# Query and key projections of two linear-attention layers as seven block products over pairs of token tiles, with the weight sums kept in DRAM

## The chip, the cores and the metric

The kernel runs on one core of one Trainium2 chip. The metric is the device time of one execution in microseconds (us); a profile of one execution of each kernel was also taken, and its "span" is a little shorter than the timed execution. Ratios between two kernels are the mean time of one kernel's fast runs over the mean of the other's fast runs of the same rounds, so they are not quite the ratio of the medians that are quoted. The times of "before" drift by up to 2.3 us between the chips that the batches ran on, so I compare ratios first and spans second.

## The reference

Two rounds of two blocks on x of shape (1, 2048, 1024): a linear attention with 32 heads of 32, and a gated bilinear layer of width 3584. Cut to what matters:

```python
def _A_ref(x, wqkv, wo):                       # linear attention; runs twice
    q, k, v = split(x @ wqkv)                  # x is layer-normalised; 32 heads of 32
    phi = lambda t: jnp.where(t > 0, t + 1, jnp.exp(t)) + 1e-6
    pq, pk = phi(q), phi(k)
    kv = jnp.einsum("bhsd,bhse->bhde", pk, v)
    z = jnp.einsum("bhsd->bhd", pk)            # sum of the keys over the tokens
    o = (pq @ kv) / (pq . z + 1e-6)
    return o @ wo
def _B_ref(x, w_gate, w_up, w_down):           # runs twice
    return ((x @ w_gate) * (x @ w_up)) @ w_down

x = x + A(layernorm(x)); x = x + B(layernorm(x))
x = x + A(layernorm(x)); x = x + B(layernorm(x))
```

I call the two attention blocks "layer one" and "layer two". In each the order of stages is: projections of q and k (with phi), state products, output products. After each come a first gate/up pass, a first down pass, and a second of both.

## The kernel before

Tokens are cut into 16 tiles of 128. For every tile and each half (512 columns) of q and k, eight 128x512 matmuls run into one PSUM bank; phi then needs one exponential on ACT (ScalarE), and a clamp and a combination on DVE (VectorE). A running sum of the keys for z is added up on Pool (GpSimd).

```python
def phi_evac(bank, dst_ap, dst_rng, eng):               # eng is "dve" everywhere
    er = R(O_E[r], 2048)                                # f32 buffer
    act:  e.activation(etmp[r], psb(bank), AF.Exp)
    eng:  e.tensor_scalar(out=etmp[r], in0=etmp[r], scalar1=1.0, scalar2=1e-6, op0=ALU.min, op1=ALU.add)
    dve:  e.scalar_tensor_tensor(out=dst_ap, in0=psb(bank), scalar=0.0, in1=etmp[r], op0=ALU.max, op1=ALU.add)

def proj(w, base, i, h, dst, r_dst, eng):
    pe:   [e.matmul(psb(bank), xnT[:, k, i*128:(i+1)*128], w[:, k, h*512:(h+1)*512], ...) for k in range(8)]

def proj_k(i, h):
    proj(wk, ...)()
    pool: e.tensor_tensor(out=za, in0=za, in1=pk[:, h, i, :], op=ALU.add)     # sum of keys, f32
...
for kind, i in seq:                                     # k tile i and q tile i-2, alternating
    ...                                                 # layernorm steps of later tiles in between
    if first and i >= 3:
        pack()                                          # DRAM to DRAM: gate/up weights into a dense order,
                                                        # 28 packings in all, 2 x 256 KB each
```

(The excerpt is shortened: buffers and dependency ranges are cut.) The first gate/up pass then runs 28 units on a ring of five weight slots; it loads each packed unit, makes its block sums on DVE and stores them for later passes, and also prepares the down weights. So its DMA engines have much to do.

## Time and profile before

1485.99 us, median of 3 runs (1485.0 to 1490.21). What matters:

| stage | us in the profile |
|---|---|
| layer one, first projection to first state product | 8.0 to 119.0 |
| layer one, output products begin | 192.4 |
| first gate/up pass | 248.5 to 417.7 |
| layer two, projections | 756.6 to 860.2 |
| layer two, output products begin | 930.5 |

The first lines of the page of the kernel before (busy time of each engine, share of the span and number of instructions; then the chain of waits that ended last, by engine):

```profile
span 1483.7 us, 20453 instructions
...
PE 1462.0 (99%) x7597; PEld 730.2 (49%) x7662; DVE 1148.6 (77%) x2122; ACT 538.7 (36%) x1096; POOL 214.2 (14%) x239
...
PE 79%; DVE 11%; DMA 5%; issue 2%; POOL 1%; ACT 1%; SPq 0%; DVEq 0%; ACTq 0%; POOLq 0%
```

TensorE never rests. The groups view of layer two's projections (line, engine, operation, shapes, count; then busy us and mean ns of one; then the engine's idle time before them and who ended it), first of a window that covers TensorE, then of DVE alone:

```profile
L740 PE MATMUL ps<-arena 128*128 128x512 bf16 x471 | 103.3, 379 | 0.5
```

```profile
L574 DVE SCALAR_TENSOR_TENSOR arena<-ps,arena 128x512 bf16<-128x512 f32 x59 | 40.8, 692 | 2.0
L572 DVE TENSOR_SCALAR arena<-arena 128x512 f32<-128x512 f32 x59 | 32.9, 558 | 17.1 <-ACT arena L571 16.4
```

One matmul lasts 379 ns from its issue to its end, but they overlap: 480 in 103.6 us is one every 0.2158 us. L574 reads PSUM and takes 0.69 us. L572 is the clamp.

The windows view (busy us of each engine and the number of instructions in a stretch, then the granted TensorE clock as a share of full speed, the DMA engines' busy share and GB/s):

```profile
756.60:860.20 103.60, 103.13 (x473) 46.96 (x481) 83.94 (x141) 35.22 (x59) 43.53 (x44) 1.00 0.45 134
...
249.90:417.70 167.80, 167.70 (x777) 71.11 (x779) 127.57 (x282) 65.82 (x112) 1.84 (x5) 1.00 0.86 274
```

DVE is busy for 83.9 of 103.6 us beside layer two's projections, and the DMA engines for 86% of the first gate/up pass. Both are second to TensorE, but not by far.

### The profile page before, as it was taken

To read this page: it belongs to the slowest core of one execution; us is meant where nothing else is said; L and a number is where in the kernel's file an instruction comes from. 1 tells how busy PE (TensorE), PEld (TensorE's weight loads), DVE (VectorE), ACT (ScalarE), POOL (GpSimd) and SP (SyncE) were. 2 spreads that over 40 slices of the span, in tenths; PEclk is the share of its full clock that TensorE was granted. 3 is DMA by queue.
4 is the path that set the end of the run, shared out by engine and by line. 5 is a ranking of instruction groups with operands and counts; after the bars stand their busy time and mean duration, and the time that the engine had idled before them with its cause. 6 is when DMAs were issued, how large, how long until landed. Compare 5 with 4: busy or idle time off the path is not lost.

```text
span 1483.7 us, 20453 instructions
## 1 busy us (share of the span) xinstructions
PE 1462.0 (99%) x7597; PEld 730.2 (49%) x7662; DVE 1148.6 (77%) x2122; ACT 538.7 (36%) x1096; POOL 214.2 (14%) x239
## 2 busy tenths in 40 slices
PE   8999999999999999999999999999999999999999
PEld 4444444444444455554444444446666445666544
DVE  7985977877756599986578768789888675888853
ACT  3332246333310244550013323466666004666400
POOL 4542721000000000000034336210000000000000
PEclk9999999999999999999999999999999999999999
DMA  8799757888875668866364337677665656666642
GB/s 269 136 177 250 159 127 173 262 267 269 264 259 191 203 238 256 264 222 234 125 213 125 117 105 151 180 165 231 244 235 192 241 198 218 237 240 224 208 172 97
DMA packets 268338, 301.76 MB, mean 203 GB/s; under 512 B 161616, under 2 KB 214608, under 8 KB 268240
## 3 DMA queue, kind: packets, MB, share of 16 engines
q1 hardware_dynamic: 268240, 300.47, 66.9%
q8 instruction: 60, 0.98, 0.3%
q14 instruction: 38, 0.31, 0.1%
HBM read 225.97 MB, written 65.54 MB: 196 GB/s over the span
## 4 chain that ended last, share of the span: by engine, by line
PE 79%; DVE 11%; DMA 5%; issue 2%; POOL 1%; ACT 1%; SPq 0%; DVEq 0%; ACTq 0%; POOLq 0%
PE ps L991 29%; PE ps L1250 23%; PE ps L740 13%; PE ps L1064 10%; DMA arena<-arena 3%; PE ps L824 3%; DVE arena L652 2%; DVE arena L760 2%; DVE arena L425 2%; DVE arena L763 2%; DVE arena L655 1%; POOL arena L769 1%; DMA arena<-w_scratch 1%; PE ps L912 1%; DVE arena L765 1%
## 5 line engine op out<-in xcount | busy, mean ns | idle before, releaser
L991 PE MATMUL ps<-arena 128*128 128x512 f16 x2240 | 530.5, 379 | 1.3 <-DMA arena<-w_scratch 0.5
L655 DVE SCALAR_TENSOR_TENSOR arena<-ps,arena 128x512 f16<-128x512 f32 (+2 forms) x564 | 373.7, 685 | 191.9 <-PE ps L1250 144.5
L652 DVE TENSOR_TENSOR arena<-arena 128x512 f16<-128x512 f16 (+6 forms) x868 | 398.8, 493 | 46.2 <-ACT arena L1068 31.6
L1250 PE MATMUL ps<-arena 128*128 128x512 f16 (+1 forms) x1548 | 338.0, 379 | 1.1
L991 PEld LDWEIGHTS ps<-arena 128*128 128x128 f16 (+1 forms) x2240 | 213.1, 98 | 214.8 <-ACT arena L996 13.6
L1250 PEld LDWEIGHTS ps<-arena 128*128 128x128 f16 x1568 | 153.4, 98 | 183.9
L740 PE MATMUL ps<-arena 128*128 128x512 bf16 x1003 | 222.8, 379 | 5.9 <-DMA arena<-arena 2.2
L1064 PE MATMUL ps<-arena 128*128 128x256 f16 x1568 | 219.0, 273 | 2.3 <-ACT arena L1068 1.9
L1064 PEld LDWEIGHTS ps<-arena 128*128 128x128 f16 (+1 forms) x1568 | 149.0, 98 | 87.4 <-ACT arena L1068 13.6
L1068 ACT ACTIVATE arena<-ps 128x256 f32<-128x256 f32 x448 | 153.4, 382 | 76.6 <-PE ps L1064 73.0
L996 ACT ACTIVATE arena<-ps 128x512 f32<-128x512 f32 x224 | 133.7, 597 | 100.2 <-PE ps L991 93.4
L1017 ACT COPY ps<-ps 128x512 f32<-128x512 f32 x112 | 63.9, 570 | 289.4 <-PE ps L991 289.4
L571 ACT ACTIVATE arena<-ps 128x512 f32<-128x512 f32 x128 | 76.3, 597 | 240.2 <-PE ps L740 220.8
L740 PEld LDWEIGHTS ps<-arena 128*128 128x128 f16 x1024 | 99.1, 98 | 125.0 <-DMA arena<-arena 5.0
L824 PE MATMUL ps<-arena 128*128 128x512 bf16 x500 | 114.6, 379 | 0.6
L912 PE MATMUL ps<-arena 128*128 128x512 bf16 x502 | 110.7, 379 | 2.4 <-ACT ps L906 1.8
L428 POOL TENSOR_SCALAR arena<-arena 128x1 f32<-128x1 f32 x64 | 20.8, 326 | 597.6 <-DVE arena L427 597.6
L425 DVE BATCH_NORM_STATS2 arena<-arena 128x6 f32<-128x512 bf16 x128 | 88.1, 688 | 11.0 <-DMA arena<-in_A_x_dram 6.0
L574 DVE SCALAR_TENSOR_TENSOR arena<-ps,arena 128x512 bf16<-128x512 f32 x128 | 88.5, 692 | 4.4
L769 POOL TENSOR_TENSOR arena<-arena 128x1024 f16<-128x1024 f32 x32 | 77.6, 2425 | 96.3 <-DVE arena L767 79.9
L572 DVE TENSOR_SCALAR arena<-arena 128x512 f32<-128x512 f32 x128 | 65.8, 514 | 33.0 <-ACT arena L571 32.1
L752 POOL TENSOR_TENSOR arena<-arena 128x512 f32<-128x512 f32 x60 | 74.6, 1248 | 90.0 <-DVE arena L574 88.6
(48 smaller groups left out, 499.2 us busy)
## 6 DMA issues: line engine op xcount, KB each, us to landing
arena<-w_scratch SPq DMA_DIRECT2D x84, 896.0 KB, 6.3
arena<-t_scratch SPq DMA_DIRECT2D x32, 896.0 KB, 6.3
arena<-in_B_w_down_dram SPq DMA_DIRECT2D x24, 896.0 KB, 6.7
w_scratch<-arena SPq DMA_DIRECT2D x28, 512.0 KB, 7.1
arena<-sp_scratch SPq DMA_DIRECT2D x28, 512.0 KB, 3.6
arena<-in_A_wqkv_dram SPq DMA_DIRECT2D x12, 1024.0 KB, 9.4
arena<-w_scratch SPq DMA_DIRECT2D x28, 384.0 KB, 5.9
x_scratch<-arena SPq DMA_DIRECT2D x36, 256.0 KB, 7.1
```

What stands on the lines that cost most here:

```text
L425: P.add("dve", (lambda h: lambda e: e.bn_stats(st[j][:, 6 * h:6 * h + 6], x_res[:, i, (D // 2) * h:(D // 2) * (h + 1)]))(h), rd=r_x(i, (D ...
L652: P.add("dve", lambda e: e.tensor_tensor(out=out, in0=a, in1=b, op=op), rd=rd, wr=wr, prd=prd)
L655: P.add("dve", lambda e: e.scalar_tensor_tensor(out=out, in0=a, scalar=sc, in1=b, op0=ALU.mult, op1=op1), rd=rd, wr=wr, prd=prd)
L740: return [e.matmul(psb(bank), xnT[:, k, i * 128:(i + 1) * 128], w[:, k, h * 512:(h + 1) * 512], start=(k == 0), stop=(k == KT - 1)) for k ...
L769: P.add("pool", lambda e: e.tensor_tensor(out=asb[b].rearrange("p (h c) -> p h c", c=32), in0=pbuf.rearrange("p (h c) -> p h c", c=32), in ...
L824: return [e.matmul(psb(bank), xr[:, t, j * 128:(j + 1) * 128], pk[:, h, t, :], start=(t == 0), stop=(t == NST - 1)) for t in range(NST)]
L912: return [e.matmul(psb(bank), xnT[:, g, i * 128:(i + 1) * 128], wp[:, g, dh * 512:(dh + 1) * 512], start=(dh == 0 and g == 0), stop=(g == ...
L991: P.add("pe", lambda e: [e.matmul(psb(bank), w[:, k, :], x[:, k, :], start=(start and k == 0), stop=(k == 3), skip_group_check=True) for k ...
L996: P.add("act", lambda e: e.activation(t, psb(bank), AF.Copy, scale=SG), prd=[bank], wr=r)
L1064: P.add("pe", lambda e: [e.matmul(psb(bank)[:, 256 * half:256 * half + 256], w[:, k, :], xx[:, k, :], start=(start and k == 0), stop=(k == ...
L1068: P.add("act", lambda e: e.activation(dst, psb(bank)[:, 0:256], AF.Copy, scale=SG), prd=[bank], wr=rd_)
L1250: return [e.matmul(psb(bank), hv[:, 7 * hf + k, t * 128:(t + 1) * 128], w[:, k, :], start=(start and hf == 0 and k == 0), stop=(hf == 1 an ...
```

## The change

The intent: a pair of token tiles (two blocks of rows), the two halves of the model width (two blocks of the contraction) and the two halves of the output form a 2x2 block product. In the Winograd form of Strassen's algorithm it takes seven block products instead of eight. Such a "quad" replaces 32 matmuls by 28. It needs four sums of the token blocks (on DVE, for each pair), four sums of the weight blocks (made once in layer one, for k on DVE and for q on Pool, stored in DRAM, and loaded back for layer two), and copies of partial results out of PSUM. Layer one does its first 8 token tiles plainly and 7 quads after them; layer two does 15 quads. The diff, cut to its core (`...` marks cuts):

```diff
+    NPL1 = 8                  # token tiles done plainly in layer one
+    LNX = (3, 5, 6)           # extra layernorm steps there
+    RLB = (7, 4)
-    O_E = [RE + i * 2048 for i in range(3)]
+    O_E = [RE + 4096 + i * 1024 for i in range(3)] + [RC + 2 * SZ_W]     # now bf16
+    kqscr = nc.dram_tensor("kq_scratch", (2, 5, 128, 2048), F16, kind="Internal").ap()
...
+        def e_min(ev, er):
+            P.add("dve", lambda e: e.tensor_scalar(out=ev, in0=ev, scalar1=1.0, scalar2=PHI0, op0=ALU.min, op1=ALU.add), rd=er, wr=er)
+        def phi_out(bank, ev, er, dst_ap, dst_rng, rl_=None):
+            e_min(ev, er)
+            if rl_:                        # layer one: relu of the bank was taken by ACT
+                rv, rr = rl_
+                tt(dst_ap, rv, ev, ALU.add, rr + er, dst_rng)
+                return
+            P.add("dve", lambda e: e.scalar_tensor_tensor(out=dst_ap, in0=psb(bank), scalar=PHI1, in1=ev, op0=ALU.add, op1=ALU.max), ...)
...
+        def s_make(tok, p):                # the four sums of the token blocks of pair p
+            return [... for o, x, y, op in ((s1, a21, a22, ALU.add), (s2, s1, a11, ALU.subtract),
+                                            (s3, a11, a21, ALU.subtract), (s4, a12, s2, ALU.subtract))]
...
+            class Quad:
+                def mm(self, q):           # four matmuls each; X, Z, Y are PSUM banks
+                    bank = {1: self.X, 6: self.X, 7: self.X, 4: self.X, 2: self.Z, 5: self.Y, 3: self.Y}[q]
+                    ...
+                    if q == 1:
+                        P.add("act", lambda e: e.copy(psb(self.Z), psb(self.X)), prd=[self.X], pwr=[self.Z])
+                def cp_u(self, j):         # a partial result out of PSUM
+                    P.add("act", lambda e: e.copy(d, psb(self.X)), prd=[self.X], wr=r)
+                def t1(self, j):           # dve: psb(Y) + PHI1 + u -> t1sb, f16
+                def out1(self, j, i, h):
+                    e_min(ev, er)
+                    tt(d, t1sb[k], ev, ALU.max, R(O_T1[k], 1024) + er, rd_)
...
-                if first and i >= 3:
-                    pack()
+                if i >= 3 and kind == "k":
+                    pack()                 # 5 beside the plain tiles
...
+                    c, m = 9 - max(NPL - 3, 0), len(items)
+                    if (n + 1) * c // m > n * c // m:
+                        job(n, 3, pack)    # 4 beside the quads
...
-                if first and n < 4:
+                if first and n % 2 == 0:
                     pack()                 # 8 in the state products (before: 4)
...
+                if first and u % 2 == 0:
+                    pack()                 # the last 11 in the first gate/up pass (before: none)
```

Two side effects belong to it: the exponential goes to bf16, and the value weights are loaded only when the last quad's buffers are free.

## The prediction

> **What bounds it now.** TensorE: the page has PE busy 1462.0 of 1483.7 us (99%), clock full in every slice. In the timeline, layer two's 480 projection matmuls take 103.6 us, one per 0.2145 us. The Trainium skill ("TensorE: Matmul & The Clock Gate", Back-to-back issue gap) gives 216 ns for the isolated gap; the trace agrees: only fewer matmuls help. Layer one's stage takes 108.4 us (10.7 to 119.1), about 5 idle, mostly waits on DMA transposes while the DMA engines are 96% busy packing weights.
>
> **Removed.** A quad replaces 32 matmuls by 28. 7 quads in layer one and 15 in layer two save 88 x 0.2145 = 18.9 us (6.0 and 12.9), all on the chain of waits.
>
> **Added.** ACT per quad: a PSUM copy (570 ns), two copies out and four exponentials (597 each): 4.2 us, plus a relu in layer one: 4.8. A quad is 6.0 us of PE, so ACT fits. VectorE: the f32 clamp (514 ns mean, 556 in layer two) becomes bf16. The skill ("VectorE: DVE Perf Modes", the perf-mode tier table) gives a 16-bit tensor_scalar twice the f32 rate; this trace has no bf16 clamp, so I estimate 0.28 us, 0.35 beside Pool traffic. PSUM reads stay at 0.69; 16-bit 128x512 tensor_tensor is 0.42. A layer-two quad: 4x0.35 + 4x0.69 + 2x0.42 = 5.0 us; 15 make 75, token sums 12, layernorm 9: 96 us of VectorE against 90 of PE. VectorE (81% busy there now) becomes the limit in the first third, where layernorm falls: 5 us given back. In layer one's quads the two are even.
>
> **Moved.** 15 packings leave layer one's projections; 4 MB of sum stores enter just before the quads, in the queue of the transposes that the next pairs need: 2 idle us recovered, 3 lost. The value weights come about 12 us before their first product; 1 MB took 9.4 us to land: 0 to 2 us lost per layer. Eleven packings go into the first gate/up pass, whose DMA is already 86% busy (168 us). One costs about 2.6 us (estimate: 16 packings in 59 us, less transposes and weights): 29 us more, near saturation. The slot ring leads by some 25 us; I charge 2. Exponential buffers no longer overlap the norm buffers: 1 us per layer won.
>
> **Sum.** Layer one -5, layer two -8, norm overlap -2, value weights +1.5, packing +2: -11.5 us. Predicted **1474 us**, 80% range **1465 to 1483**. Faster by over 2% (below 1456): 0.02; within 2%: 0.96; slower by over 2%: 0.02.
>
> **What would show it.** PE instructions down by 88. Layer two's stage (first projection to first state matmul) 94 to 98 us: near 90 would say VectorE never held it, 103 that it ate the gain. VectorE above 95% busy in its first half, TensorE waiting for it. Clamp near 0.3 us in the groups view. Layer one's stage 101 to 106, its waits naming DMA after the plain half. First gate/up pass 168 to 172 us, DMA above 95%. Other stages within 1 us.
>
> **What would make it wrong.** A clamp much slower than 0.35 us, or Pool holding VectorE off (single clamps now reach 1.2 us). A product waits for ACT's copy of the same bank: a late ACT stalls TensorE in each quad, 0.3 us per quad would cost 7 us. Saturated DMA starving the ring: up to 10 us. The other way, if VectorE catches up during the first state products, the whole 19 us arrives: 1466.

## The result, and the profile after

| | median us | runs | ratio to before (95%) |
|---|---|---|---|
| before | 1487.43 | 4 (1485.0 to 1490.21) | |
| after | 1488.85 | 4 (1487.4 to 1491.32) | 1.0011 (0.9992 to 1.0029) |

The same time: of the 18.9 us of matmuls that the prediction counted, nothing shows in the total. The lines of the page of the kernel after:

```profile
span 1487.0 us, 20482 instructions
...
PE 1451.5 (98%) x7512; PEld 720.7 (48%) x7574; DVE 1182.1 (79%) x2218; ACT 595.3 (40%) x1201; POOL 234.0 (16%) x256
...
PE 69%; DVE 18%; DMA 7%; issue 3%; SPq 1%; ACT 1%; POOL 1%; DVEq 0%; ACTq 0%
```

The weight loads (PEld) fell by 88, as they should: the matmuls are gone. The chain of waits shows what took their place: DVE's share of it rose from 11% to 18%, DMA's from 5% to 7%, and TensorE's fell from 79% to 69%.

Where it went, by stage, from the timelines of both traces:

| stretch | before | after | difference | predicted |
|---|---|---|---|---|
| start to layer one's output products | 192.4 | 196.3 | +3.9 | -5 |
| layer one's output products | 56.1 | 55.3 | -0.8 | 0 |
| first gate/up pass | 169.2 | 172.6 | +3.4 | +2 |
| to layer two's first projection | 338.9 | 339.3 | +0.4 | 0 |
| layer two, to its output products | 173.9 | 170.1 | -3.8 | -8 |
| rest | 553.2 | 553.4 | +0.2 | 0 |
| span | 1483.7 | 1487.0 | +3.3 | -11.5 |

(In the column of the prediction, the 2 us for norm overlap and the 1.5 us for value weights are left out of the rows and stand in the sum only.)

**Layer two.** The windows and the groups view of the kernel after:

```profile
763.50:783.50 20.00, 18.64 (x85) 7.86 (x85) 16.13 (x35) 10.39 (x18) 6.17 (x10) 1.00 1.12 299
783.50:803.50 20.00, 16.74 (x71) 6.30 (x71) 19.48 (x41) 10.54 (x19) 8.41 (x11) 1.00 0.30 80
803.50:823.50 20.00, 18.78 (x83) 7.78 (x84) 19.55 (x41) 11.95 (x21) 7.57 (x7) 1.00 0.62 184
823.50:843.50 20.00, 19.70 (x90) 8.78 (x92) 19.56 (x38) 13.37 (x24) 8.24 (x7) 1.00 0.00 0
```

```profile
L606 DVE TENSOR_SCALAR arena<-arena 128x512 bf16<-128x512 bf16 x55 | 27.4, 498 | 1.0 <-ACT arena L610 1.0
L628 DVE SCALAR_TENSOR_TENSOR arena<-ps,arena 128x512 bf16<-128x512 f32 x28 | 19.4, 692 | 1.0
```

From 783 us on DVE is busy 19.5 of every 20 us, and TensorE starts 71 matmuls in a stretch that has room for 93. The projections end at 863.8 (the last ones are mixed with 16 state products, which I take off at 0.2158 us each), so they take 100.3 us where their matmuls need 90.6. The bf16 clamp (L606) takes 0.498 us on average. Its median is 0.286 and its maximum 1.25: it is two populations (17 of the 55 took over 0.6 us; of the 59 f32 clamps of the kernel before it was 15), and the timeline shows what the slow one does. Start, duration, engine, line:

```profile
788.93 0.42 DVE L757 TENSOR_TENSOR arena<-arena 128x512 f16<-128x512 f16 x1
...
789.10 1.26 POOL L869 TENSOR_TENSOR arena<-arena 128x512 f32<-128x512 f32 x1 [1.95 <-DVE arena L628]
789.26 1.25 DVE L606 TENSOR_SCALAR arena<-arena 128x512 bf16<-128x512 bf16 x1
```

Pool begins to add a key tile to z at 789.10 and ends at 790.36; the clamp that DVE issued at 789.26 ends at 790.51, 0.15 us after Pool. The Trainium skill ("SBUF — State Buffer", SBUF: two separate sides) says that DVE instructions in a two-port mode, or with two SBUF inputs while Pool's instruction reads SBUF too, and Pool's instructions share one pair of ports under an exclusive lock: whichever starts first has it, and the other "fully blocks". The trace agrees: L628, which reads one operand from PSUM, took 0.69 us every time (0.691 to 0.692).

**Layer one.** TensorE's timeline where the plain half ends and the quads begin (start, duration of the merged piece, idle time before it and what ended it):

```profile
60.65 10.52 PE L878 MATMUL ps<-arena 128*128 128x512 bf16 x47 [0.56 <-DMA arena<-arena]
71.00 1.03 PE L907 MATMUL ps<-arena 128*128 128x512 bf16 x4
78.52 4.81 PE L907 MATMUL ps<-arena 128*128 128x512 f16 x12 [6.49 <-DVE arena L757]
85.77 38.97 PE L907 MATMUL ps<-arena 128*128 128x512 f16 x169 [2.44 <-DVE arena L676]
```

The first quad (L907) starts, then waits 6.5 us for the token sums (L757) and 2.4 us for the last weight sum (L676), both on DVE. The windows view of the same place shows the granted clock (third column from the right) fall:

```profile
70.00:75.00 5.00, 2.03 (x10) 0.71 (x8) 4.83 (x13) 2.13 (x5) 4.49 (x6) 1.00 0.58 120
75.00:80.00 5.00, 1.48 (x4) 0.59 (x5) 4.83 (x10) 0.53 (x2) 2.64 (x4) 0.59 1.09 325
80.00:85.00 5.00, 3.33 (x9) 1.01 (x7) 4.96 (x6) 1.67 (x3) 3.87 (x4) 0.73 0.19 79
85.00:90.00 5.00, 4.23 (x12) 1.64 (x13) 4.86 (x10) 1.16 (x2) 2.44 (x3) 0.66 0.64 232
```

Between 75 and 90 us 25 matmuls kept TensorE busy for 9.0 us instead of 5.4. DVE is full all the time. The quads of layer one end at 126.3 (again taking off 16 mixed state products): 55.3 us for 196 matmuls that need 42.3. The plain half before them also got longer: the first quad starts at 71.0, while the kernel before had loaded the weights of as many matmuls (256) by about 67.4. No run isolates these 3.6 us; the trace has 1.9 us of TensorE waits for DMA transposes in that half, and a clock of 0.65 and 0.50 from 7 to 11 us. DVE's costliest clamp and addition there, in the groups view (8 to 71 us):

```profile
L757 DVE TENSOR_TENSOR arena<-arena 128x512 bf16<-128x512 f16 x27 | 16.4, 607 | 2.1 <-ACT arena L619 1.3
L606 DVE TENSOR_SCALAR arena<-arena 128x512 bf16<-128x512 bf16 x27 | 14.2, 526 | 1.3 <-ACT arena L610 1.0
```

**First gate/up pass.** The windows view of it, and who DVE waited for in it:

```profile
251.60:424.20 172.60, 170.34 (x782) 71.00 (x782) 127.69 (x286) 66.89 (x114) 2.58 (x6) 1.00 0.98 294
```

```profile
DVE arena L757 <- DMA arena<-w_scratch: 15.4, 9, 2.5
DVE arena L757 <- DMA arena<-in_B_w_down_dram: 15.0, 9, 2.3
```

The DMA engines went from 86% to 98% busy, and the weight preparation waits 30 us for loads there, where the waits view of the kernel before shows none. In the plain half, meanwhile, they were nearly idle (DMA share 0.15, before 0.60):

```profile
40.00:60.00 20.00, 18.57 (x91) 8.39 (x90) 19.59 (x28) 9.77 (x18) 18.92 (x17) 1.00 0.15 28
```

So there were three theories to test. **A**: layer one loses where the quads begin ("the seam"), because DVE is behind. **B**: in layer two DVE is full because Pool's sums block the clamps; rivals: the burst of layernorm in the first third (B2), or ACT's copies between the products (B3). **C**: the packings moved into the gate/up pass fill the DMA queue there.

### The profile page after: what moved, and what is told of

Read it like the earlier page. It is cut to its first block, busy times and chain, and to the rows that moved or that the text cites. A ratio compares the mean times of both kernels' runs of the same rounds, so it can differ in the third digit from the quotient of the medians.

```text
span 1487.0 us, 20482 instructions
## 1 busy us (share of the span) xinstructions
PE 1451.5 (98%) x7512; PEld 720.7 (48%) x7574; DVE 1182.1 (79%) x2218; ACT 595.3 (40%) x1201; POOL 234.0 (16%) x256
## 4 chain that ended last, share of the span: by engine, by line
PE 69%; DVE 18%; DMA 7%; issue 3%; SPq 1%; ACT 1%; POOL 1%; DVEq 0%; ACTq 0%
PE ps L1566 22%; PE ps L1307 21%; PE ps L1380 10%; PE ps L1125 7%; DVE arena L757 6%; DMA arena<-in_B_w_down_dram 5%; PE ps L1228 3%; PE ps L907 3%; DVE arena L606 3%; DVE arena L445 3%; DVE arena L760 2%; PE ps L878 2%; DMA arena<-arena 1%; DVE arena L929 1%; DVE arena L628 1%
## 5 line engine op out<-in xcount | busy, mean ns | idle before, releaser
L757 DVE TENSOR_TENSOR arena<-arena 128x256 f32<-128x256 f32 (+6 forms) x999 | 465.8, 495 | 81.1 <-ACT arena L1384 31.6
L1566 PE MATMUL ps<-arena 128*128 128x512 f16 (+1 forms) x1548 | 338.0, 379 | 1.1
L1566 PEld LDWEIGHTS ps<-arena 128*128 128x128 f16 x1568 | 153.5, 98 | 183.9
L1312 ACT ACTIVATE arena<-ps 128x512 f32<-128x512 f32 x224 | 133.7, 597 | 103.6 <-PE ps L1307 91.8
L907 PE MATMUL ps<-arena 128*128 128x512 f16 (+1 forms) x606 | 140.9, 387 | 15.5 <-DVE arena L757 8.3
L1125 PE MATMUL ps<-arena 128*128 128x512 bf16 x498 | 114.7, 379 | 0.7
L1228 PE MATMUL ps<-arena 128*128 128x512 bf16 x502 | 110.5, 379 | 1.8 <-ACT ps L1222 1.3
L907 PEld LDWEIGHTS ps<-arena 128*128 128x128 f16 x616 | 59.1, 99 | 96.5 <-issue 10.6
L1228 PEld LDWEIGHTS ps<-arena 128*128 128x128 f16 x512 | 50.0, 98 | 62.0 <-ACT ps L1222 2.1
L878 PE MATMUL ps<-arena 128*128 128x512 bf16 x312 | 72.2, 385 | 4.9 <-DMA arena<-arena 1.9
L1125 PEld LDWEIGHTS ps<-arena 128*128 128x128 f16 x512 | 49.2, 98 | 55.7
```

The source lines that it names most:

```text
L757: P.add("dve", lambda e: e.tensor_tensor(out=out, in0=a, in1=b, op=op), rd=rd, wr=wr, prd=prd)
L878: return [e.matmul(psb(bank), xnT[:, k, i * 128:(i + 1) * 128], t[:, k, h * 512:(h + 1) * 512], start=(k == 0), stop=(k == KT - 1)) for k ...
L907: P.add("pe", lambda e: [e.matmul(psb(bank), a[0][:, k, :], b[0][:, k, :], start=(q in (1, 5) and k == 0), stop=(k == 3), skip_group_check ...
L1125: return [e.matmul(psb(bank), xrt[t][:, jj * 128:(jj + 1) * 128], pk[:, h, t, :], start=(t == tok[0]), stop=(t == tok[NST - 1])) for t in ts]
L1228: return [e.matmul(psb(bank), xnT[:, g, i * 128:(i + 1) * 128], wp[:, g, dh * 512:(dh + 1) * 512], start=(dh == 0 and g == 0), stop=(g == ...
L1312: P.add("act", lambda e: e.activation(t, psb(bank), AF.Copy, scale=SG), prd=[bank], wr=r)
```

## The experiments

Twelve kernels ran. One of them gave a wrong result; all the others were correct. No ratio is 2% away from 1. I call a kernel faster or slower than "before" where its interval leaves out 1; the changed kernel was not run again in these batches, and only combo and its two variants are clearly below its interval. What single changes won is therefore read from the lengths of stages, in one profile each. The milestones, from TensorE's timeline (differences of starts rounded to 0.1 us):

| kernel | ratio (95%) | output 1 begins | gate/up pass | layer two, projections to output | span |
|---|---|---|---|---|---|
| before | 1 | 192.4 | 169.2 | 173.9 | 1483.7 |
| after | 1.0011 (0.9992, 1.0029) | 196.3 | 172.6 | 170.1 | 1487.0 |
| l1_plain | 1.0098 (1.0083, 1.0114) | 203.3 | 175.4 | 169.0 | 1496.9 |
| l1_12 | 1.0027 (1.001, 1.0044) | 194.4 | 175.5 | 169.1 | 1488.0 |
| l2_no_z | 0.9985 (0.9969, 1.0001) | 197.0 | 172.2 | 163.9 | 1480.6 |
| packs_early | 1.006 (1.0041, 1.0078) | 208.4 | 169.8 | 169.3 | 1495.2 |
| packs_fill | 0.9988 (0.9973, 1.0002) | 196.5 | 169.6 | 169.0 | 1482.7 |
| light_l2 | 0.9992 (0.9975, 1.0009) | 197.2 | 172.3 | 164.8 | 1482.4 |
| light_l1 | 0.9979 (0.9964, 0.9994) | 190.1 | 172.1 | 169.1 | 1479.0 |
| combo | 0.9905 (0.9889, 0.9921) | 188.3 | 169.1 | 164.9 | 1470.2 |
| l1_plain_v | 1.0091 (1.0076, 1.0106) | 204.1 | 176.3 | 169.1 | 1499.2 |
| combo_nf | 0.9916 (0.9902, 0.9929) | 189.6 | 168.8 | 165.4 | 1472.9 |
| combo_xz | 0.9919 (0.9906, 0.9933) | 186.5 | 169.0 | 165.4 | 1469.6 |
| l1_plain_w | 1.0025 (1.0004, 1.0047) | 196.4 | 174.9 | 169.0 | 1489.5 |

If the 60 matmuls less of layer two's quads all counted, its column would show 161.0 (173.9 less 60 times 0.2158). Seven of the kernels (l1_plain, l1_12, packs_early, packs_fill, light_l1, l1_plain_v, l1_plain_w) have the changed kernel's layer two; they show 169.0 to 169.3 there, the changed kernel's own profile 170.1. One profile is thus good to about 1 us, and I give what is gained in layer two as a range over both: 8.1 to 9.1 us are lacking.

### l1_plain: no quads in layer one

```diff
-    NPL1 = 8
+    NPL1 = 16
-                if i >= 3 and kind == "k":
+                if i >= 3 and kind == "k" and (i < 8 or i % 2):
                     pack()
```

> No quads in layer one (all 16 token tiles plain), the same 17 packings before the first gate/up pass, layer two as in the changed kernel. Theory A, that layer one loses about 13.6 us where the quads begin (6.5 and 2.4 us of TensorE waits for VectorE and about 4.7 us of half clock after them) against 6.0 us saved: about 7.5 us faster than the changed kernel, 1481 us, no wait over 2 us in layer one's projections, clock 1.00 in every window there. Rival: layer one lost its time to the making of the weight sums and the Pool work beside the plain tiles, which stay here: no faster than 1487.

Measured 1499.75 us, 1% slower. The projections themselves went well: they ended at 121.0, 5.3 us sooner than with the quads. But then:

```profile
PE ps L1151 <- DMA arena<-in_A_wqkv_dram: 9.6, 1, 9.6
```

Without quads the value weights are loaded only after the stage, and the first value product waited 9.6 us. My edit had moved a load. This run says nothing about the total.

### l1_12: the quads begin later

```diff
-    NPL1 = 8
+    NPL1 = 12
```

> Layer one's quads begin at token tile 12 instead of 8, so the layernorm of all tiles is nearly done by then; 3 quads left instead of 7 (2.6 us saved instead of 6.0). Theory A, that the wait at the seam comes from VectorE still having layernorm and exponentials in front of the first token sums: the first wait shrinks below 2 us, no half clock, total about 1480. Rival, that the seam costs the same wherever it is put (weight sums, stores, POOL's last four subtractions): wait still 6 us or more, total 1490 or more.

Measured 1489.58 us, neither as good as A said nor a repetition of the full seam. The timeline:

```profile
98.35 3.73 PE L907 MATMUL ps<-arena 128*128 128x512 bf16 x15
106.06 15.79 PE L907 MATMUL ps<-arena 128*128 128x512 f16 x59 [3.98 <-DVE arena L676]
```

With the layernorm behind it the wait of 6.5 us for token sums is gone, as A said, but the wait for the last weight sum (L676) grew to 4.0 us, and the clock still fell to 0.50 in 106 to 110. The output products began 1.9 us earlier than in the changed kernel; the gate/up pass was 2.9 us longer and took it back. I made the last weight sum earlier in combo because of this run.

### l2_no_z: Pool's sums left out in layer two

```diff
-                else:
+                elif first:
                     P.add("pool", lambda e: e.tensor_tensor(out=za, in0=za, in1=pa, op=ALU.add), ...)
```

The result is wrong.

> Wrong result on purpose: in layer two the running sum of the keys is not added up on Pool after the first tile (30 additions of 1.2 us less). Theory B, that VectorE is full there because one clamp in four or five waits for a Pool addition to end (mean 0.50 instead of 0.28 us): clamp mean falls to 0.30 us, layer two's stage from 100 to about 93 us, total about 1481. Rival B2, that the layernorm burst in the first third alone overfills VectorE: the stage stays at 98 or more. Rival B3, that the copies between PSUM banks on ACT hold TensorE: no change at all.

Measured 1482.54 us. The clamp's line of the groups view for layer two's stage:

```profile
L606 DVE TENSOR_SCALAR arena<-arena 128x512 bf16<-128x512 bf16 x59 | 17.0, 287 | 7.3 <-ACT arena L610 4.7 <-ACT arena L935 2.3
```

The clamp fell from 0.498 to 0.287 us and from waiting for nobody to waiting for ACT. Layer two took 163.9 us, 5.1 to 6.2 us less, of the 8.1 to 9.1 that it lacked. No clamp took over 0.296 us any more. That Pool's sums block DVE, and that this costs 5 to 6 us, is shown. B2 or B3 have at most the 2.9 us that remain above 161.0.

### packs_early: no packing in the gate/up pass

```diff
-                if i >= 3 and kind == "k":
+                if i >= 3:
                     pack()
-                if first and n % 2 == 0:
+                if first:
                     pack()
```

(The packing in the gate/up pass is then never reached.)

> All 28 weight packings are issued before the first gate/up pass, none in it. Theory C, that eleven packings fill the DMA queue there (0.97 to 1.00 busy) and delay the slot loads: the pass shrinks from 174.7 to about 171.5 us, VectorE's 30 us of waits for w_scratch and w_down loads there go away, total about 1486. Rival: the pass is as long as before and something else grew; or the packings cost the same again in the state products: total unchanged.

Measured 1493.92 us. The pass shrank to 169.8 us, more than the 171.5 that C said. The rival's half came true too: fourteen packings in the state products filled the queue there.

```profile
PE ps L1179 <- DVE arena L1156: 8.5, 1, 8.5
```

TensorE waited 8.5 us for a mask product that comes after the value weights' last product, and layer one's output began 12 us later. DVE reached that product late: it stood in order behind normalisation steps that waited for Pool, and Pool waited 19.5 us for DMA transposes in 170 to 202 us. (The profiled run was the slowest of the four, which took 1491.0 to 1497.0 us.)

### packs_fill: packings where the DMA engines had room

```diff
-                if i >= 3 and kind == "k":
+                if i >= 3:
                     pack()
-                    c, m = 9 - max(NPL - 3, 0), len(items)
+                    c, m = len(items), len(items)
```

> Only the places of the packings change: two per token tile in the plain half from tile 3 (10 instead of 5), one per quad (7 instead of 4), 8 in the state products as before, so 3 instead of 11 are left for the first gate/up pass. Theory C, that the DMA engines had room in 40 to 60 us (0.15 busy) and 100 to 120 us (0.48) and are the limit of the gate/up pass: pass 171 us instead of 173.9, nothing lost in the state products, ratio to before 0.9985 to 0.999 (2 to 3 us better than the changed kernel). Rival, that early packings delay the layernorm transposes and the first quads as much: pass shorter, but the quads begin later; ratio 1.001 or more.

Measured 1484.12 us, 0.9988. The pass took 169.6 us, 3.0 less, and layer one's output began at 196.5 against 196.3: nothing was lost elsewhere. The pass in the windows view, and DVE's waits for loads in it:

```profile
251.70:421.30 169.60, 168.72 (x781) 71.40 (x781) 129.22 (x285) 67.21 (x114) 2.58 (x6) 1.00 0.89 281
```

```profile
DVE arena L757 <- DMA arena<-in_B_w_down_dram: 2.0, 1, 2.0
...
DVE arena L757 <- DMA arena<-w_scratch: 0.3, 1, 0.3
```

30.4 us of waits became 2.3, and the DMA share fell from 0.98 to 0.89. Theory C is shown for its size of 3 us.

### light_l2: one clamp of four on ACT, in layer two

The clamp min(exp(t), 1) is exp(min(t, 0)), which ACT can do alone: relu of -t, then the exponential of minus that. The third and fourth outputs, whose inputs are both in SBUF, take clamp and maximum in one DVE instruction.

```diff
+        def phi_neg(bank):
+            P.add("act", lambda e: e.activation(ev, psb(bank), AF.Relu, scale=-1.0), prd=[bank], wr=er)
+            P.add("act", lambda e: e.activation(ev, ev, AF.Exp, scale=-1.0), rd=er, wr=er)
...
-                    self.e[bank] = phi_exp(bank) + ...
+                    self.e[bank] = phi_neg(bank) if rl["lt"] and bank in RLB else phi_exp(bank) + ...
...
-                    e_min(ev, er)
-                    tt(d, t1sb[k], ev, ALU.max, ...)
+                        P.add("dve", lambda e: e.scalar_tensor_tensor(out=d, in0=ev, scalar=1.0, in1=t1sb[k], op0=ALU.min, op1=ALU.max), ...)
```

> Layer two only: the clamp of one of the four outputs of a quad goes to ACT (relu of minus t, then exp of minus that), and the last two outputs take clamp and maximum in one VectorE instruction; Pool's sums stay. Theory B, that VectorE with Pool's blocking is the limit of layer two's quads: about 1 us of VectorE less per quad, stage from 100 to about 93 us, ratio 0.996. Rival B2, the layernorm burst: stalls stay in the first third, stage 98. Rival B3, ACT's copies between the products hold TensorE: ACT gets 0.7 us more per quad, so the stage gets longer, 101 or more.

Measured 1484.63 us, 0.9992 (0.9975 to 1.0009). Layer two took 164.8 us, 4.2 to 5.3 less than with the changed kernel's layer two. The ratio missed the 0.996 that was expected: it is 0.0019 (2.8 us) below the changed kernel's, with overlapping intervals. ACT got more work and the stage still got shorter, so ACT was not the limit of the changed kernel (B3 falls at this dose), and the stalls did not stay (B2 falls as the main cause). But one part of the edit did not do what I thought:

```profile
L958 DVE SCALAR_TENSOR_TENSOR arena<-arena 128x512 bf16<-128x512 bf16 x29 | 28.0, 965 | 1.6 <-ACT arena L949 1.6
```

The fused instruction takes 0.68 us alone and 0.965 on average: with two operands in SBUF it waits for Pool too.

### light_l1: the same in layer one

The edit of light_l2 with the switch on layer one, and for the plain tiles as well:

```diff
         def phi_evac(bank, dst_ap, dst_rng):
+            if rl["lt"]:
+                ev, er, n_ = phi_neg(bank)
+                phi_out(bank, ev, er, dst_ap, dst_rng, n_)       # no clamp: one PSUM read on DVE
+                return
```

> The same lightening in layer one only, for the plain half's outputs too (one PSUM read on VectorE at 0.69 us in place of clamp and add, 0.53 + 0.61 us beside Pool). Theory A, that VectorE's backlog makes the 6.5 us wait at the first quad: wait under 3 us, clock at 1.00, output stage begins 5 to 8 us earlier. Theory C, that the DMA engines set the end of the first gate/up pass: of that gain at most 2 us are left when the pass ends (it ends near 424 us in the profile whatever came before), ratio 1.000. Rival to C: the gain goes through, ratio 0.997 or lower.

Measured 1483.36 us, 0.9979. TensorE at the seam:

```profile
72.03 2.14 PE L921 MATMUL ps<-arena 128*128 128x512 bf16 x8
74.85 1.90 PE L921 MATMUL ps<-arena 128*128 128x512 f16 x8 [0.68 <-ACT ps L924]
79.55 38.97 PE L921 MATMUL ps<-arena 128*128 128x512 f16 x169 [2.79 <-DVE arena L690]
```

The wait of 6.5 us is gone; the one for the last weight sum (L690 here) is left, and the clock of 1.00 that was expected did not come: it was 0.67 in 80 to 85 us. The output products began 6.2 us earlier than in the changed kernel, within what A said. The part of C that I had added is refuted: the pass began 5.9 us earlier, again took 172.1 us, and so ended at 417.8. The packings lengthen the pass, but they do not pin its end.

### combo: all of it

Both of the edits above in both layers, packs_fill, and

```diff
-                if kind == "q" and i >= 1 and len(twk) > 1:
+                if kind == "q" and i >= 1 and (len(twk) > 1 or (twk and i >= NPL - 2)):
                     twk.pop(0)()                 # the last weight sum of k before the last two q tiles
```

> Both layers lightened, packings moved as in packs_fill, and the keys' third weight sum made before the last two query tiles. If theories A, B and C hold, the gains add and the one of layer one is no longer swallowed: layer one 5 to 8 us, the pass 3, layer two 7: ratio 0.989 to 0.992, 1470 to 1474 us, faster than both kernels. If one of them is wrong its part is missing.

Measured 1471.4 us, ratio 0.9905 (0.9889 to 0.9921): faster than the kernel before, by a ratio that also lies below the changed kernel's interval, and inside what was expected. The spans of the profiles add up: the three parts alone are 4.3, 4.6 and 8.0 us below the changed kernel's, together 16.9, and combo is 16.8 below it. The ratios add less neatly (0.0074 from the parts, 0.0106 for combo); light_l1's profiled run was its fastest, 2.1 us under its median, so the neat sum of the spans is partly luck. The intervals and the earlier weight sum can account for the rest, and I did not resolve it. At the seam two waits are left, and the clock still drops once:

```profile
74.18 1.04 PE L921 MATMUL ps<-arena 128*128 128x512 f16 x4 [1.21 <-DVE arena L771]
75.90 40.71 PE L921 MATMUL ps<-arena 128*128 128x512 f16 x177 [0.68 <-ACT ps L924]
```

```profile
75.00:80.00 5.00, 4.32 (x14) 1.55 (x13) 4.93 (x8) 1.90 (x4) 4.37 (x4) 0.66 1.02 250
```

### l1_plain_v: no quads in layer one, second try

```diff
+                if kind == "q" and i == 8 and NPL == NST:
+                    ...                          # store the weight sums
+                    load_v(0)
+                    load_v(1)
```

> The earlier run without quads in layer one (l1_plain) missed through my own edit: with no quads the value weights were loaded only after the stage, and the first value product waited 9.6 us for them. Here they are loaded from query tile 8 on. Theory A: the output stage of layer one begins at about 192 us in the profile, 4 us before the changed kernel's 196.3, because the seam of the quads costs more (about 13 us) than they save (6.0); ratio 0.998 to 0.999. Rival, that layer one's loss lies in the weight sums and the Pool work, which stay: 196 or later, ratio 1.001 or more.

Measured 1499.46 us: a miss again. All DMAs are issued from one queue in order. The value loads had to wait until the stores of the sums had left the same buffers, and a layernorm transpose stood behind them:

```profile
98.40 32.84 PE L878 MATMUL ps<-arena 128*128 128x512 bf16 x144 [7.95 <-DMA arena<-arena]
```

### combo_nf: combo without the fused instruction

```diff
-                        P.add("dve", lambda e: e.scalar_tensor_tensor(out=d, in0=ev, scalar=1.0, in1=t1sb[k], op0=ALU.min, op1=ALU.max), ...)
+                    e_min(ev, er)
+                    tt(d, t1sb[k], ev, ALU.max, ...)
```

> combo without the fused clamp and maximum. In combo's trace that fused instruction takes 0.96 us on average (0.68 when nothing is in its way), as much as the two instructions that it replaces (0.50 + 0.43). If it waits for Pool[...], fusing was worth nothing: within 1.5 us of combo, ratio 0.990 to 0.991. If fusing did carry combo's gain in layer two, this one loses 3 us or more: ratio 0.993.

Measured 1472.82 us, 0.9916 against combo's 0.9905, the intervals overlapping; layer two 165.4 against 164.9. Fusing was worth nothing that can be told apart here. By elimination, layer two's gain came from the one clamp in four that left DVE for ACT.

### combo_xz: two clamps of four on ACT

```diff
-                    self.e[bank] = phi_neg(bank) if rl["lt"] and bank in RLB else ...
+                    self.e[bank] = phi_neg(bank) if rl["lt"] and (bank in RLB or not first) else ...
```

> combo_nf with the clamp of both directly read banks of a layer-two quad on ACT. Theory B: VectorE loses another 0.5 us per quad and layer two's stage gets to its matmul time, about 161 us from first projection to first output product (combo 165, before 174); ratio 0.987 to 0.989. Rival B3: ACT is now at 5.6 of 6.0 us per quad and its copies hold the products; stage 166 or longer, ratio 0.991 or more.

Measured 1472.63 us, 0.9919; layer two 165.4 us, no better. The waits of weight loads in that stage name ACT's copy (L928):

```profile
PEld ps L921 <- ACT arena L928: 8.1, 15, 1.2
```

In combo_nf the same line of the waits view has 3.7 us. So at this dose the waits speak for B3: from 794 us on DVE is busy 17.6 to 17.7 of 20 us (in combo_nf 18.4 to 19.4), and ACT's copies hold the products. No run took work off ACT to test it. About 4 us above the 161.0 are left in layer two; what else they hold I did not find out.

### l1_plain_w: no quads in layer one, third try

```diff
+                if kind == "q" and i in (5, 6, 7) and NPL == NST:
+                    for w in "kq":
+                        tw_store(w, {5: 1, 6: 2, 7: 4}[i])
+                if kind == "q" and i in (10, 12) and NPL == NST:
+                    load_v(i // 2 - 5)
```

> Third try at layer one without quads. The second (l1_plain_v) missed again through my edit: the value loads waited in the issuing queue for the weight-sum stores and held up a layernorm transpose behind them for 8 us. Here the stores go out at query tiles 5, 6 and 7 and the loads at 10 and 12, so that nothing waits. Theory A: output stage of layer one begins at 191 to 193 us in the profile (changed kernel 196.3, kernel before 192.4), so the four quad pairs of layer one cost more than they save; ratio 0.998 to 0.9995. Rival: the quads are worth their 6 us and the loss is in the sums and Pool work beside them: 197 us or later, ratio 1.002 or more.

Measured 1490.47 us, 1.0025, with layer one's output products at 196.4. The projections ended at 122.5, 3.8 us sooner than with the quads; the state stage gave that back (there TensorE waited 2.5 and 1.2 us for DVE). The kernel before, though, waited 2.8 us at the same products (2.4 of it for DVE), and its state stage was as long: 73.4 us against 73.9 here and 70.0 in the changed kernel. So in the changed kernel the quads of layer one are worth nothing up to the output products, neither the gain of 6 us nor the loss that A expected. And without any quads layer one is still 4.0 us behind the kernel before; that is nearer to the rival, which put the loss beside the quads. Weight sums, ACT's extra relu, the new order and the moved packings are all still there, and which of them costs it was not separated. The evidence is thin: the four runs spread from 1487.2 to 1492.0 us, the profile is of one of the slow ones, and TensorE waited 2.7 us for a DMA transpose before 62.3 us, so the hope that nothing would wait was not quite met. The gate/up pass was also 2.3 us longer than in the changed kernel; in all four runs with fewer quads it was longer (174.9 to 176.3 against 172.6), and why is open. What did help layer one was less work on DVE, in light_l1.

## Why the prediction was wrong

The prediction was 1474 us; the measured median was 1488.85, outside the range of 1465 to 1483, and the change made no difference. In the profile -11.5 us had been predicted and +3.3 came; of these 14.8 us, 8.9 lie in layer one's row of the table, 4.2 in layer two's and 1.4 in the pass.

- **Right: 88 matmuls less.** 88 weight loads less are on the page. That layer two would get DVE-limited was right too, but not only "in the first third": DVE is busy 19.5 of every 20 us from 783 us to the end of the stage, and 9.7 us were given back (100.3 less 90.6) where 5 had been charged.
- **Right in mechanism, wrong in size: "0.28 us, 0.35 beside Pool traffic" for the clamp.** Alone it takes 0.286 us, just as estimated with the Trainium skill ("VectorE: DVE Perf Modes", the perf-mode tier table), which has a 16-bit tensor_scalar at twice the f32 rate. Beside Pool it averaged 0.498 us. I had the evidence in the profile before: the f32 clamp was 0.558 us on average at a median of 0.427, so 0.13 us of it was blocking, and single clamps took 1.2 us. The blocking costs up to a whole Pool instruction (1.2 us), whatever the clamp itself costs, and the shorter clamp did not make it rarer: 17 of 55 against 15 of 59. Against the 0.35 us of the sum, 60 clamps at 0.15 us more are 8.9 us of DVE; against the free clamp, fifty-five clamps at 0.21 us more are 11.7 us of an engine that had none to spare. l2_no_z took the blocking away and got 5 to 6 us back. The kernel before could afford it: its DVE had 20 of 104 us idle.
- **Wrong: "Layer one -5".** It was +3.9. The step that failed is the claim that only the first quads would lose 3 us, for DMA, and that DVE and TensorE are even in layer one's quads. The waits named DVE, not DMA: 6.5 and 2.4 us, plus a granted clock of 0.59 to 0.73, which my sum did not have at all. The 2 us that were to be recovered in the plain half did not come either; it got 3.6 us longer. That DVE came to the seam behind is shown by light_l1, which puts one instruction that reads PSUM in place of the clamp and the addition of the plain half, and brought the output stage forward by 6.2 us. That Pool's blocking made it late there too (clamp 0.526 us instead of 0.286, the addition after it 0.607 instead of 0.42) fits, but no run took Pool's work out of layer one; and l1_plain_w loses 4.0 us with no seam at all, so how the loss divides stays open.
- **Right in mechanism, a little small: "packing +2".** It was +3.4 us, with the DMA engines at 98% as foretold; packs_fill took 3.0 of it back. What I did not ask is whether the packings could have stayed where the engines were at 15%.
- **Wrong, but in its favour: value weights.** I charged 1.5 us; no wait for them shows in the changed kernel.
- **Norm overlap -2: not tested.** The state stages were 3.4 and 0.5 us shorter than before (70.0 and 69.8 us), but no run tells whether the exponential buffers did it.
- **"What would make it wrong" named the cause.** "Pool holding VectorE off (single clamps now reach 1.2 us)" stood there as a risk, without a number in the sum. It cost 5 to 6 us in layer two, more than any other single term that a run measured there. The risk that a late ACT stalls TensorE cost 1.3 us of waits in the changed kernel's layer two, not 7.

What stays open: the 4 us that layer two's projections keep above their matmul time in the best version, how much of the clock's fall at the seam can be avoided, how layer one's loss divides between the seam and the work beside the quads, and whether the lightened DVE work would help the kernel before without the block products (not run; there DVE was not the limit of layer two).

## What to carry to other kernels

When an engine that is second in line is 80% busy, a change that speeds up the first one can turn the second into the limit, as here; then its durations have to be taken as they are beside its neighbours, with the blocked population counted, not the median of the undisturbed one. Where Pool runs long SBUF instructions beside VectorE, try the form that reads PSUM, or move the work to ACT: here an instruction of 0.69 us that was not blocked in the traces beats two of 0.28 and 0.42 that were. And when a change moves transfers, look for the stretch where the DMA engines are idle, not only for one that no compute waits on.

## What the Trainium skill lacked or had wrong

- "SBUF — State Buffer" (SBUF: two separate sides) has the exclusive lock between VectorE and GpSimd, and the trace agrees: 0.286 us became up to 1.25 us beside a Pool addition of 1.2 us. What it lacks is an average cost to plan with: here, with two Pool additions of 1.2 us per key tile, a clamp took 0.498 us on average, and 0.287 without the additions.
- "VectorE: DVE Perf Modes" (the perf-mode tier table) has no row for scalar_tensor_tensor, and no page gives a time for it. From SBUF with 16-bit operands it took 0.68 us for 512 elements (the rate of the PSUM form, 0.69 us), against 0.42 us for a 16-bit tensor_tensor. So fusing two instructions into one won nothing.
- "TensorE: Matmul & The Clock Gate" (HAM oscillation) gives the rule of no idle gaps above about 3.4 us, and tells further on that frequent short idle times can also throttle the clock, without a length. In combo the longest idle gaps at the seam were 1.2 and 0.7 us, close together, and the clock still fell to 0.66 in 75 to 80 us; in l1_plain_w gaps of 2.5 and 1.2 us left it at 1.00 in 186 to 198 us.
- The same page (Back-to-back issue gap) gives 131 ns per matmul of 512 columns as the sustained rate in a stream of weight loads and matmuls. Here 480 of them at full clock took 103.6 us in the kernel before, 0.2158 us each, which is the page's isolated figure of 216 ns.
